# Where the cache slots start in SBUF, and which DMA engines take the last row of wo

## The chip, the cores and the metric

The kernel runs on one core of one Trainium2 chip. The metric is the device time of one execution, in microseconds (us), as the median of several. Executions of this kernel agree within about 0.1%.

## The reference

It is one decode step. The costly part is attention of one query token over a long cache; around it are two layer norms, a small MLP and a gate.

```python
B, Sq, D = 2, 1, 512
Hq, Hkv, Sk, Dh = 32, 8, 32768, 128       # k_cache, v_cache: [B, Hkv, Sk, Dh], bf16

q = (xn @ wq).reshape(B, Sq, Hq, Dh).transpose(0, 2, 1, 3)
k, v = repeat(k_cache, 4, axis=1), repeat(v_cache, 4, axis=1)
p = softmax(einsum("bhqd,bhkd->bhqk", q, k) * Dh ** -0.5)
s = einsum("bhqk,bhkd->bhqd", p, v).transpose(0, 2, 1, 3).reshape(B, Sq, Hq * Dh) @ wo
g = silu(mlp(xn))                          # mlp: w1 to w4 ... (cut)
return x + s * g
```

The two caches are 268 MB. Every byte is read once, so the kernel is a stream from HBM with some arithmetic beside it.

## The kernel before

Each load of the cache is 4 MB. It lands in one of five rotating "slots" of 32 KB in each of the 128 partitions. The same slots take wq, w3 with w4, and at the end wo. A pool gives its tiles addresses in the order in which pools are opened, so the 19 KB of small tiles in `pers` come first and the slots begin behind them.

```python
    pers = ctx.enter_context(tc.tile_pool(name="pers", bufs=1))
    slots = ctx.enter_context(tc.tile_pool(name="slots", bufs=SLOTS))     # SLOTS = 5
    ktp = ctx.enter_context(tc.tile_pool(name="ktp", bufs=T_BUFS))
    # ... more pools

    def slot(name):
        return slots.tile([128, SLOT], BF16, tag="slot", name=name)       # SLOT = 16384

    def load_cache(cache, b, g, i, name):
        t = slot(name)
        nc.sync.dma_start(
            out=t[:, :],
            in_=cache[b, g, i * NK:(i + 1) * NK, :].rearrange("(p t) d -> p (t d)", p=128),
        )
        return t
```

The prologue issues six loads one after another (wq, k0, k1, w3, w4, v0). From then on each load waits for a slot to be free.

```python
    wo_parts = [(0, RW // 2), (RW // 2, RW - 4), (RW - 4, RW - 1), (RW - 1, RW)]   # RW = 32
    for n in range(NW + 1):                   # NW = 32 pairs of k and v loads
        if n + 2 < NW:
            k_tiles[n + 2] = load_cache(A_k_cache, *work[n + 2], "k")
        if 0 < n + 1 < NW:
            v_tiles[n + 1] = load_cache(A_v_cache, *work[n + 1], "v")
        if n == NW - 1:
            wo_t = slot("wo")
            wo3 = wo_t[:, 0:Hq * D].rearrange("p (r c) -> p r c", r=RW)
            wos = A_wo.rearrange("(p r) d -> p r d", r=RW)
            for a, z in wo_parts:
                nc.sync.dma_start(out=wo3[:, a:z, :], in_=wos[:, a:z, :])
        # ... transposes, scores, exp, and the weighted sum of v
    # ... then 128 matmuls of oX with wo3, row by row, and the output
```

wo has 32 rows of 1 KB in each partition. It comes in four pieces of 16, 12, 3 and 1 rows, so that little is left to multiply once the last one lands.

The softmax here doesn't subtract the row's maximum and nothing guards it: scores larger than these inputs give would overflow.

Of the kernel before, what the change touches and what calls it, by code (L numbers as in the profile page):

```python
# [9 lines left out]
BF16 = mybir.dt.bfloat16  # L10
# [9 lines left out]
SLOTS = 5  # L20
# [6 lines left out]
def kernel(  # L27
# [14 lines left out]
    nc = tc.nc  # L42

    B, Sq, D = A_x.shape
# [18 lines left out]
    QW = D // NQ  # L63
    QP = 32 * (NQ - 1) + B
    RW = HD // 128
    RQ = Dh // RW

    pers = ctx.enter_context(tc.tile_pool(name="pers", bufs=1))
    slots = ctx.enter_context(tc.tile_pool(name="slots", bufs=SLOTS))
    ktp = ctx.enter_context(tc.tile_pool(name="ktp", bufs=T_BUFS))  # L70
    epp = ctx.enter_context(tc.tile_pool(name="epp", bufs=2))
    ptp = ctx.enter_context(tc.tile_pool(name="ptp", bufs=3))
# [7 lines left out]
    def slot(name):  # L80
        return slots.tile([128, SLOT], BF16, tag="slot", name=name)
# [8 lines that stand above are left out]
# [6 lines left out]
        out=wq_t[:, 0:DK * HD],  # L96
        in_=A_wq.rearrange("(p k) f -> p (k f)", k=DK),
    )

    x4_bf = pers.tile([128, QW], BF16)  # L100
    nc.gpsimd.memset(x4_bf[:, :], 0.0)
    for n in range(NQ):
        nc.gpsimd.dma_start(out=x4_bf[32 * n:32 * n + B, :], in_=A_x[:, 0, n * QW:(n + 1) * QW])
# [18 lines left out]
    for j in range(4):  # L122
        nc.vector.tensor_copy(
            out=sel[:, :, :, j, :],
            in_=ident[:, :].rearrange("p (b w e) -> p b e w", b=NB, e=2),
# [4 lines left out]
        out=sel_o[:, :, :],  # L130
        in_=ident[:, :].rearrange("p (j a t h) -> p a t h j", j=4, t=VT, h=rep)[:, 0, :, :, :],
# [4 lines left out]
        out=sel_h[:, :],  # L136
        in_=ident[:, :].rearrange("p (r h) -> p h r", h=rep),
# [4 lines left out]
    with nc.allow_low_precision(reason="sums of zeros and a single one"):  # L142
        nc.vector.tensor_reduce(
            out=sel_r[:, :],
            in_=ident[:, :].rearrange("p (q r) -> p r q", r=RW),
# [4 lines left out]
        out=mask[:, :],  # L150
        in_=ident[:, :].rearrange("p (q r) -> p q r", r=RW),
# [48 lines left out]

    onx = pers.tile([128, B, Hq, RQ], BF16)

    oX = pers.tile([128, RW, B], BF16)
    g4 = pers.tile([128, QW], F32)
    x4 = pers.tile([128, QW], F32)
    nc.gpsimd.tensor_copy(out=x4[:, :], in_=x4_bf[:, :])
# [14 lines left out]
    for nb in range(NB):  # L221
# [9 lines left out]
        out=qr[:, :, :, :, :].rearrange("p n e b h -> p (n e b h)"),  # L231
        in_=qr_ps[:, :, :, :].rearrange("p n e c -> p (n e c)"),
# [56 lines left out]
    def emit_k(n):  # L289
        b, g, i = work[n]  # L290
        if i == 0:
            state["z"] = emit_z(b, g)
        z = state["z"]
        kt = k_tiles.pop(n)[:, :].bitcast(I32)
        sc = sc_ps.tile([128, RT * 32], F32, tag="sc", name="sc")
        W = RT * NB * 32
        for r in range(NR):
            T = ktp.tile([128, W], I32, tag="T", name="T")
            nc.vector.transpose(  # L299
                out=T[:, :].rearrange("p (b t k) -> p t b k", b=NB, t=RT),  # L300
                in_=kt[:, r * W:(r + 1) * W].rearrange("p (t b k) -> p t b k", b=NB, t=RT),
            )
            Tb = T[:, :].bitcast(BF16).rearrange("p (b c e) -> p b c e", b=NB, e=2)
            zc = (NR - 1 - r) * rep
            for nb in range(NB):
                for e in range(2):
                    nc.tensor.matmul(  # L307
                        sc[:, :],
                        lhsT=z[:, nb, e, zc:zc + 128],
                        rhs=Tb[:, nb, :, e],  # L310
                        start=(r == 0 and nb == 0 and e == 0),
                        stop=(r == NR - 1 and nb == NB - 1 and e == 1),
                    )
        ep = epp.tile([128, RT * 32], BF16, tag="ep", name="ep")
        rs = smp.tile([128, 1], F32, tag="rs", name="rs")
        nc.scalar.activation(out=ep[:, :], in_=sc[:, :], func=ACT.Exp, scale=inv_sqrt_dh, accum_out=rs[:, :])  # L316
        pt = ptp.tile([128, NR, RT * rep], BF16, tag="pt", name="pt")
        nc.vector.transpose(  # L318
            out=pt[:, :, :].rearrange("p r (t h) -> p t r h", h=rep),
            in_=ep[:, :].rearrange("p (t r h) -> p t r h", r=NR, h=rep),  # L320
        )
        return pt, rs
# [46 lines left out]
                )  # L369
                nc.vector.tensor_copy(out=oX[:, :, b], in_=xp[:, :])  # L370

    wo_parts = [(0, RW // 2), (RW // 2, RW - 4), (RW - 4, RW - 1), (RW - 1, RW)]
    NW = len(work)
    eps = {}
    for n in range(NW + 1):
# [5 lines that stand above are left out]
            wo_t = slot("wo")  # L381
            wo3 = wo_t[:, 0:Hq * D].rearrange("p (r c) -> p r c", r=RW)
            wos = A_wo.rearrange("(p r) d -> p r d", r=RW)
            for a, z in wo_parts:
                nc.sync.dma_start(out=wo3[:, a:z, :], in_=wos[:, a:z, :])  # L385
        if n < NW:
            eps[n] = emit_k(n)
        if n == 1:
            emit_mlp()
        if n > 0:  # L390
            emit_v(n - 1, eps.pop(n - 1))
# [16 lines left out]
    for b, eng in ((0, nc.sync), (1, nc.scalar)):  # L408
        eng.dma_start(
            out=out[b, 0, :].rearrange("(n c) -> n c", c=QW),  # L410
            in_=out4[b:QP:32, :],
# [31 lines left out]
```

## Time and profile before

| | before |
|---|---|
| time, median | 665.06 us |
| span in the profile | 663.4 us |
| share of 16 DMA engines' span, queue of the loads | 98.6% |
| rate between 50 and 600 us | 431 GB/s |
| PE, DVE busy | 62%, 52% |
| where the slots start | 35872 B = 70 x 512 + 32 |

The address is from the built program. The slots are 32768 B apart, so all five start 32 B past a multiple of 512.

In the profiles PE is the engine of the matrix products and PEld its loading of weights; DVE, ACT and POOL are the vector, scalar and general engines, and SP issues the loads. A q after a name (SPq) is that engine's instruction queue. L307 is line 307 of the kernel. PEclk is the clock that PE was granted, as a share of full speed.

First the profile's page of the kernel before: part 1 gives the engines' busy time (and share of the span), part 2 the DMA's rate in 40 slices, part 3 the DMA queues with packets, MB and share of 16 engines, part 4 the chain of waits that ended last, by engine and line.

```profile
span 663.4 us, 6213 instructions
PE 411.3 (62%) x2622; PEld 172.7 (26%) x2622; DVE 344.8 (52%) x422; ACT 50.1 (8%) x152; POOL 7.0 (1%) x20
...
GB/s 380 419 433 440 428 426 437 427 432 435 422 435 428 431 434 429 430 435 428 433 431 428 433 426 435 432 427 434 427 434 431 424 437 430 425 439 428 429 430 203
...
q1 hardware_dynamic: 10232, 280.50, 98.6%
q8 instruction: 20, 0.33, 0.2%
...
DMA 75%; PE 16%; DVE 6%; issue 2%; ACT 0%; SPq 0%; DVEq 0%; ACTq 0%
DMA k<-in_A_k_cache_dram 69%; PE sc L307 13%; DMA wo<-in_A_wo_dram 6%; DVE T L299 5%; PE o L339 3%; DVE pt L318 1%; ACT ep L316 0%; PE S L335 0%; PE s_ps L397 0%; DVE sm L334 0%; SPq L95 0%; SPq L385 0%; DVE sg L405 0%; DVE out L407 0%; DVEq L299 0%
```

Read it from the queue: q1 has something to move nearly always, and no compute engine is close to full. The chain says the same. The windows table of the kernel before, for the long middle stretch, has the engines' busy time, the granted clock, the DMA share and GB/s as its last three numbers:

```profile
core 0: us, PE busy (x) PEld busy (x) DVE busy (x) ACT busy (x) POOL busy (x), PEclk, DMA share, GB/s
50.00:600.00 550.00, 351.12 (x2027) 142.63 (x2025) 293.98 (x346) 40.14 (x124) 0.00 (x0) 0.78 1.00 431
```

A DMA share of 1.00 means that the engines never idle here. Only two things can shorten this stretch: fewer bytes, or less time for each packet. The DMA issues of the kernel before show the four pieces of wo (KB each, then us from issue to landing), and the last steps of its chain show what follows the landing (start, us, what):

```profile
wo<-in_A_wo_dram SPq DMA_DIRECT2D x1, 2048.0 KB, 34.6
wo<-in_A_wo_dram SPq DMA_DIRECT2D x1, 1536.0 KB, 37.9
wo<-in_A_wo_dram SPq DMA_DIRECT2D x1, 384.0 KB, 38.4
wo<-in_A_wo_dram SPq DMA_DIRECT2D x1, 128.0 KB, 38.3
```

```profile
619.16 37.85 DMA wo<-in_A_wo_dram
657.01 0.04 issue
657.05 1.91 PE s_ps L397 x64
658.96 0.02 issue
658.98 0.30 DVE sg L405
```

Last, the packets themselves. The trace has one record for each, with queue, start, duration and size, but not the DMA engine; which packets share an engine is inferred, here and below, from one starting where another ends (within a few ns: most often 3 or 4 ns before it). Some 32 KB packets take 1.6 to 1.9 us: each of the 24 of them after the first 40 us starts within 20 ns of the end of an instruction packet (18 of queue q8, 6 of q14). These "interrupted" ones are left out. Counted over the others, more than 50 us after the first:

```
kernel before: 7757 packets, mean 1217.9 ns
  1216 ns 56%   1224 ns 22%   1215 ns 9%   1221 ns 6%   ...
before about 33 us: 338 of the uninterrupted ones take 1213 ns
```

### The profile page before, as it was taken

The page shows a single profiled execution, that of the slowest core. Times are in us where ns is not written, and L with a number is a line of the kernel's source. Part 1 is how long each engine was busy: PE and PEld are TensorE (multiplying, and loading weights), DVE is VectorE, ACT ScalarE, POOL GpSimd, SP SyncE. Part 2 cuts the span into 40 slices and gives each one's busy share as a digit, 9 for nine tenths or more (in the row PEclk, how much of TensorE's full clock was granted, in tenths as well). Part 3 has the DMA queues.
Part 4 walks back from the last instruction along what each step waited for, and adds up shares of the span by engine and source line. Part 5 has one row for each costly group of instructions (what it writes and reads, how often), then busy time and mean ns, then how long its engine had stood idle before and what let it go on. Part 6 is the DMA issues. An engine that isn't in the chain of part 4 may idle for free.

```text
span 663.4 us, 6213 instructions
## 1 busy us (share of the span) xinstructions
PE 411.3 (62%) x2622; PEld 172.7 (26%) x2622; DVE 344.8 (52%) x422; ACT 50.1 (8%) x152; POOL 7.0 (1%) x20
## 2 busy tenths in 40 slices
PE   2585667576468755567665655766565576764574
PEld 2242223222123322223222222322222232221222
DVE  4563456554445655445656444565644466554450
ACT  1111100000000000000000000000000000000000
POOL 3000000000000000000000000000000000000000
PEclk9985898667887867788876779887678987778886
DMA  9999999999999999999999999999999999999994
GB/s 380 419 433 440 428 426 437 427 432 435 422 435 428 431 434 429 430 435 428 433 431 428 433 426 435 432 427 434 427 434 431 424 437 430 425 439 428 429 430 203
DMA packets 10528, 280.89 MB, mean 423 GB/s; under 512 B 1403, under 2 KB 1541, under 8 KB 1669
## 3 DMA queue, kind: packets, MB, share of 16 engines
q1 hardware_dynamic: 10232, 280.50, 98.6%
q8 instruction: 20, 0.33, 0.2%
q0 software_dynamic: 256, 0.01, 0.0%
q14 instruction: 8, 0.06, 0.0%
q10 hardware_dynamic: 12, 0.00, 0.0%
HBM read 280.50 MB, written 0.00 MB: 423 GB/s over the span
## 4 chain that ended last, share of the span: by engine, by line
DMA 75%; PE 16%; DVE 6%; issue 2%; ACT 0%; SPq 0%; DVEq 0%; ACTq 0%
DMA k<-in_A_k_cache_dram 69%; PE sc L307 13%; DMA wo<-in_A_wo_dram 6%; DVE T L299 5%; PE o L339 3%; DVE pt L318 1%; ACT ep L316 0%; PE S L335 0%; PE s_ps L397 0%; DVE sm L334 0%; SPq L95 0%; SPq L385 0%; DVE sg L405 0%; DVE out L407 0%; DVEq L299 0%
## 5 line engine op out<-in xcount | busy, mean ns | idle before, releaser
L307 PE MATMUL sc<-T,z 128*128 128x512 bf16 x1024 | 300.4, 460 | 190.3 <-DVE T L299 190.0
L299 DVE STREAM_TRANSPOSE T<-k 128x1024 int32<-128x1024 int32 x256 | 292.1, 1208 | 178.3 <-DMA k<-in_A_k_cache_dram 178.3
L307 PEld LDWEIGHTS <-z 128*128 128x128 bf16 x1024 | 114.1, 111 | 375.1 <-issue 293.8
L339 PE MATMUL o<-v,pt 128*16 128x512 bf16 x1024 | 73.7, 439 | 4.7 <-DMA v<-in_A_v_cache_dram 4.7
L318 DVE STREAM_TRANSPOSE pt<-ep 128x512 bf16<-128x512 bf16 x32 | 22.8, 711 | 77.5 <-ACT ep L316 77.5
L316 ACT ACTIVATE ep<-sc 128x512 bf16<-128x512 f32 x32 | 19.1, 597 | 536.3 <-PE sc L307 536.3
L339 PEld LDWEIGHTS <-pt 128*16 128x16 bf16 x1024 | 25.5, 98 | 41.1 <-issue 23.7
L335 PE MATMUL S<-sm,ones_f 128*128 128x4 f32 x64 | 12.0, 258 | 24.8 <-DVE sm L334 24.8
L351 PE MATMUL oT<-sel_o,ob 128*128 128x4 f32 x128 | 16.9, 255 | 11.1 <-ACT ob L348 11.1
L351 PEld LDWEIGHTS oT<-sel_o,ob 128*128 128x128 f32 x128 | 15.5, 191 | 19.5 <-ACT ob L348 19.5
L335 PEld LDWEIGHTS S<-sm,ones_f 128*128 128x128 f32 x64 | 9.7, 190 | 32.6 <-DVE sm L334 32.6
L330 DVE MEMSET o<- 128x512 f32 x16 | 7.8, 485 | 13.4 <-ACT ob L348 12.3
L283 ACT COPY z<-qr 32x16 bf16<-32x16 bf16 x64 | 12.6, 197 | 11.5 <-DVE qr L230 10.9
L358 DVE TENSOR_TENSOR on<-oT,rec 128x4 f32<-128x4 f32 x16 | 2.6, 162 | 20.0 <-PE oT L351 20.0
L348 ACT COPY ob<-o 128x512 f32<-128x512 f32 x16 | 9.4, 585 | 26.0 <-PE o L339 26.0
L356 DVE RECIPROCAL rec<-S 128x4 f32<-128x4 f32 x16 | 2.9, 183 | 7.3 <-PE S L335 7.2
L212 PE MATMUL qT_ps<-xT,wq 128*128 128x2 bf16 x128 | 3.6, 165 | 4.5 <-DMA wq<-in_A_wq_dram 4.5
L316 ACT ACTIVATION_READ_ACCUMULATOR ep<-sc 128x1 f32 x32 | 6.3, 198 | 0.2
L334 DVE TENSOR_SCALAR sm<-sel_h,rs 128x4 f32<-128x4 f32 x32 | 6.1, 189 | 0.0
L212 PEld LDWEIGHTS <-wq 128*128 128x128 bf16 x128 | 3.5, 104 | 4.6 <-DMA wq<-in_A_wq_dram 4.6
L195 PE MATMUL treg<-ident,xn_bf 2*128 2x2 bf16 x4 | 0.3, 175 | 6.8 <-DVE xn_bf L187 6.8
L397 PE MATMUL s_ps<-wo,oX 128*2 128x128 bf16 x128 | 3.0, 265 | 1.7 <-DMA wo<-in_A_wo_dram 1.4
(63 smaller groups left out, 42.0 us busy)
## 6 DMA issues: line engine op xcount, KB each, us to landing
k<-in_A_k_cache_dram SPq DMA_DIRECT2D x32, 4096.0 KB, 44.3
v<-in_A_v_cache_dram SPq DMA_DIRECT2D x32, 4096.0 KB, 39.4
wq<-in_A_wq_dram SPq DMA_DIRECT2D x1, 4096.0 KB
w<-in_B_w_dram SPq DMA_DIRECT2D x2, 1792.0 KB, 37.8
wo<-in_A_wo_dram SPq DMA_DIRECT2D x1, 2048.0 KB, 34.6
wo<-in_A_wo_dram SPq DMA_DIRECT2D x1, 1536.0 KB, 37.9
wo<-in_A_wo_dram SPq DMA_DIRECT2D x1, 384.0 KB, 38.4
wo<-in_A_wo_dram SPq DMA_DIRECT2D x1, 128.0 KB, 38.3
```

Source lines behind the costliest of these rows:

```text
L212: nc.tensor.matmul(qT_ps[:, h * B:(h + 1) * B], lhsT=wq3[:, k, h * Dh:(h + 1) * Dh], rhs=xT[:, k, :], start=(k == 0), stop=(k == DK - 1),)
L283: nc.scalar.copy(out=z[32 * j:32 * j + 32, :, :, c:c + rep], in_=qr[32 * j:32 * j + 32, :, :, b, g * rep:(g + 1) * rep],)
L299: nc.vector.transpose(out=T[:, :].rearrange("p (b t k) -> p t b k", b=NB, t=RT), in_=kt[:, r * W:(r + 1) * W].rearrange("p (t b k) -> p t ...
L307: nc.tensor.matmul(sc[:, :], lhsT=z[:, nb, e, zc:zc + 128], rhs=Tb[:, nb, :, e], start=(r == 0 and nb == 0 and e == 0), stop=(r == NR - 1 ...
L316: nc.scalar.activation(out=ep[:, :], in_=sc[:, :], func=ACT.Exp, scale=inv_sqrt_dh, accum_out=rs[:, :])
L318: nc.vector.transpose(out=pt[:, :, :].rearrange("p r (t h) -> p t r h", h=rep), in_=ep[:, :].rearrange("p (t r h) -> p t r h", r=NR, h=rep),)
L330: nc.vector.memset(state["o"][:, :], 0.0)
L334: nc.vector.tensor_scalar_mul(out=sm[:, :], in0=sel_h[:, :], scalar1=rs[:, 0:1])
L335: nc.tensor.matmul(S[:, :], lhsT=ones_f[:, :], rhs=sm[:, :], start=(i == 0), stop=(i == NPART - 1))
L339: nc.tensor.matmul(o[32 * j:32 * j + VT * rep, :], lhsT=pt[:, r, a * VT * rep:(a + 1) * VT * rep], rhs=vt[:, u * VT:(u + 1) * VT, :].rearr ...
L348: nc.scalar.copy(out=ob[:, :], in_=o[:, :])
L351: nc.tensor.matmul(oT[:, :], lhsT=ob[:, t * Dh:(t + 1) * Dh], rhs=sel_o[:, t, :], start=(t == 0), stop=(t == VT - 1),)
```

## The change

It has two parts. The first moves all of `pers` behind the slots and leaves a small pool, `head`, ahead of them. `head` holds 256 + 128 = 384 B, which brings the slots to 16896 = 33 x 512. The second splits the last piece of wo by partitions, 119 and 9, so that the DMA engines share this row unequally. The intent is shorter packets in the stream, and less work at the end for the engines that finish last.

```diff
+    head = ctx.enter_context(tc.tile_pool(name="head", bufs=1))
+    slots = ctx.enter_context(tc.tile_pool(name="slots", bufs=SLOTS))
     pers = ctx.enter_context(tc.tile_pool(name="pers", bufs=1))
-    slots = ctx.enter_context(tc.tile_pool(name="slots", bufs=SLOTS))
 ...
-    x4_bf = pers.tile([128, QW], BF16)
+    x4_bf = head.tile([128, QW], BF16)
 ...
-    oX = pers.tile([128, RW, B], BF16)
+    oX = head.tile([128, RW, B], BF16)
 ...
-    wo_parts = [(0, RW // 2), (RW // 2, RW - 4), (RW - 4, RW - 1), (RW - 1, RW)]
+    wo_parts = [
+        (0, RW // 2, 0, 128), (RW // 2, RW - 4, 0, 128), (RW - 4, RW - 1, 0, 128),
+        (RW - 1, RW, 0, 119), (RW - 1, RW, 119, 128),
+    ]
 ...
-            for a, z in wo_parts:
-                nc.sync.dma_start(out=wo3[:, a:z, :], in_=wos[:, a:z, :])
+            for a, z, p0, p1 in wo_parts:
+                nc.sync.dma_start(out=wo3[p0:p1, a:z, :], in_=wos[p0:p1, a:z, :])
```

## The prediction

What the prediction says of the hardware and no trace or run of this case shows is cut; the cuts are marked. The sum: 665.06 - 0.34 - 0.3 = 664.4 us, put at 664.2 for the chance of a larger effect of alignment. The grounds of its two terms:

- The 0.34 us of the tail rest on an assumption: that the seven engines which take the 119 partitions are the seven that end early. Each later engine would then have eight 1 KB packets less to write. In the trace of the kernel before, such packets are 46 ns long and follow each other on an engine about 43 ns apart, and eight are 0.34 us. If the assumption fails, the prediction had the change 0.4 us slower.
- Why an off start should cost anything was not shown, so this term, 0 to 1 ns per packet, is the author's estimate. The larger case, a gain of 2 to 4 us (661 to 663 us), is the one in which the later 3 and 8 ns per packet come from the off start.

> **What bounds the kernel now.** The DMA stream. The DMA table gives the cache loads' queue 98.6% of 16 engines' span; the windows table has DMA share 1.00 and 431 GB/s from 50 to 600 us, while PE is busy 62% and DVE 52% of the span (page, part 1). The chain of waits is 75% DMA. 280.5 MB at 431 GB/s is 651 of the 663.4 us.
>
> **The packets (trace's DMA records).** Each cache load is 128 packets of 32 KB, one per partition. Before about 33 us they take 1213 ns, later 1216 ns, with 1221 or 1224 ns about every fourth descriptor. Packets of 1, 3, 14 and 32 KB in the quiet phase took 46, 121, 535 and 1213 ns: a slope of 27.2 GB/s per engine (435 GB/s for 16), plus about 8 ns each. At that slope 32 KB is 1205 ns. So what is not payload in the steady stream is about 84 ns of the 9.72 us that one load takes on each engine: 0.9%, under 6 us over 67 loads. Alignment can give no more.
>
> **Alignment.** As built, every slot starts 32 B past a multiple of 512. [...] But the trace says it costs little: [...] the slots were as misaligned while packets took 1213 ns as later. I expect 0 to 1 ns less per packet, about 0.3 us in all, with some chance of 2 to 4 us[...].
>
> **The last row of wo.** Following packet chains, the engines end their last wo packets between 653 and 658 us: seven within the first microsecond, nine 3 to 5 us later, three of these in the last 0.3 us. The late ones carry more interruptions by instruction packets (16 KB, 1.07 us). [...] 0.34 us off the last to end, all on the critical path.
>
> **Sum.** 665.06 - 0.34 (tail) - 0.3 (alignment) = 664.4; with the chance of a larger alignment effect I say 664.2 us, range 662.0 to 665.2. Faster by over 2%: 0.01; within 2%: 0.98; slower: 0.01.
>
> **What would show it.** Tail: the last row's 1 KB packets on seven engines, the last engine 0.3 us earlier, the early seven 0.4 us later. Alignment: 32 KB packets still at 1213 early and 1216/1224 later, 431 GB/s mid-run. If alignment matters more, the common packet falls towards 1205 to 1213 ns and mid-run shows 433 GB/s or above.
>
> **What would make it wrong.** [...] instruction fetches landing elsewhere and moving the last engine by up to 1 us.

## The result, and the profile after

| | before | after |
|---|---|---|
| time, median | 665.13 us (665.03 to 665.48, 6 runs) | 662.20 us (662.04 to 662.58, 6 runs) |
| span in the profile | 663.4 us | 660.5 us |
| 32 KB packets, mean after the first 50 us | 1217.9 ns | 1213.0 ns |
| instruction packets of 16 KB (q8), median | 1071 ns | 935 ns |
| rate between 50 and 600 us | 431 GB/s | 433 GB/s |

The ratio is 0.9956, with a 95% interval of 0.9943 to 0.9968. A ratio here is the mean time of one kernel's runs over that of the other's of the same rounds, so it is not quite the ratio of the medians. The change saves 2.9 us, 0.4%. By the rule of 2% that is "same", but it is clear of the noise.

The page of the kernel after, the same parts:

```profile
span 660.5 us, 6182 instructions
PE 408.5 (62%) x2590; PEld 173.7 (26%) x2622; DVE 344.9 (52%) x422; ACT 50.1 (8%) x152; POOL 6.9 (1%) x20
...
GB/s 381 418 437 442 416 442 435 425 442 429 430 439 422 439 440 421 440 433 426 443 429 426 443 426 433 434 429 438 433 428 439 426 435 440 425 435 438 427 428 210
...
q1 hardware_dynamic: 10232, 280.50, 98.6%
q8 instruction: 20, 0.33, 0.2%
...
DMA 75%; PE 15%; DVE 6%; issue 2%; ACT 0%; SPq 0%; DVEq 0%; ACTq 0%
```

The shares did not move: 98.6% and 75% as before. This is how a faster stream looks when the stream is the limit. Only the rate tells, in the windows table of the kernel after:

```profile
50.00:600.00 550.00, 347.68 (x1999) 143.18 (x2026) 294.81 (x348) 40.83 (x126) 0.00 (x0) 0.77 1.00 433
```

DVE is busy as long as before (344.9 us against 344.8), so the moved tiles changed nothing for it. (PE has 2590 matmul records in place of 2622: some are missing from this trace.) The DMA issues and the end of the chain of the kernel after:

```profile
wo<-in_A_wo_dram SPq DMA_DIRECT2D x1, 2048.0 KB, 34.3
wo<-in_A_wo_dram SPq DMA_DIRECT2D x1, 1536.0 KB, 37.7
wo<-in_A_wo_dram SPq DMA_DIRECT2D x1, 384.0 KB, 38.3
wo<-in_A_wo_dram SPq DMA_DIRECT2D x1, 119.0 KB
```

```profile
617.69 38.15 DMA wo<-in_A_wo_dram
655.84 0.04 issue
655.88 0.30 PE s_ps L402 x4
656.19 0.02 issue
656.21 0.30 DVE sg L410
```

Before, the chain left the DMA with 64 matmuls to do: it waited last for the piece of 12 rows, which is 48 matmuls and is followed by 16 more. The last row was not on the chain. It was issued at 620.1 us and landed 38.3 us later, at 658.4, while its own four matmuls start only at 658.6: it had some 0.25 us in hand. After, only 4 matmuls remain, which are those of the split row. That row has become what ends last.

The packet records of the kernel after are unlike those before: 7757 uninterrupted packets of 32 KB, and to the nearest percent all of them take 1213 ns, and so do the earlier ones from about 6 us on. (In the first microseconds, as all engines start, packets are longer and scattered in both kernels, up to 2.1 us before and 2.4 us after.) The 1216 and 1224 ns are gone.

### The profile page after: what moved, and what is told of

It is laid out like the page before. It is cut to its first block, busy times and chain, and to the rows that moved or that the text cites. A ratio compares the mean times of both kernels' runs of the same rounds, so it can differ in the third digit from the quotient of the medians.

```text
span 660.5 us, 6182 instructions
## 1 busy us (share of the span) xinstructions
PE 408.5 (62%) x2590; PEld 173.7 (26%) x2622; DVE 344.9 (52%) x422; ACT 50.1 (8%) x152; POOL 6.9 (1%) x20
## 3 DMA queue, kind: packets, MB, share of 16 engines
q1 hardware_dynamic: 10232, 280.50, 98.6%
## 4 chain that ended last, share of the span: by engine, by line
DMA 75%; PE 15%; DVE 6%; issue 2%; ACT 0%; SPq 0%; DVEq 0%; ACTq 0%
DMA k<-in_A_k_cache_dram 69%; PE sc L309 11%; DMA wo<-in_A_wo_dram 6%; DVE T L301 6%; PE o L341 3%; DVE pt L320 1%; ACT ep L318 0%; PE S L337 0%; SPq L390 0%; DVE sm L336 0%; SPq L97 0%; PE s_ps L402 0%; DVE sg L410 0%; DVE out L412 0%; DVEq L301 0%
## 5 line engine op out<-in xcount | busy, mean ns | idle before, releaser
L309 PE MATMUL sc<-T,z 128*128 128x512 bf16 x992 | 295.2, 457 | 190.6 <-DVE T L301 183.3
L341 PE MATMUL o<-v,pt 128*16 128x512 bf16 x1024 | 75.5, 447 | 4.9 <-DMA v<-in_A_v_cache_dram 4.9
## 6 DMA issues: line engine op xcount, KB each, us to landing
wo<-in_A_wo_dram SPq DMA_DIRECT2D x1, 384.0 KB, 38.3
```

The source lines that it names most:

```text
L309: nc.tensor.matmul(sc[:, :], lhsT=z[:, nb, e, zc:zc + 128], rhs=Tb[:, nb, :, e], start=(r == 0 and nb == 0 and e == 0), stop=(r == NR - 1 ...
L341: nc.tensor.matmul(o[32 * j:32 * j + VT * rep, :], lhsT=pt[:, r, a * VT * rep:(a + 1) * VT * rep], rhs=vt[:, u * VT:(u + 1) * VT, :].rearr ...
```

## The experiments

Eleven kernels ran, each correct. In the table, the ratio is to the kernel before in the same rounds. "Packet" is the mean of the uninterrupted 32 KB packets more than 50 us after the first.

| run | slots mod 512 | last rows of wo | time, us (median) | ratio | packet, ns |
|---|---|---|---|---|---|
| before (665.13 to 665.33 in the four sets) | 32 | not split | 665.14 | 1 | 1217.9 |
| after | 0 | 1 row, 119 + 9 | 662.20 | 0.9956 | 1213.0 |
| align_only | 0 | not split | 662.07 | 0.9953 | 1213.0 |
| split_only | 32 | 1 row, 119 + 9 | 665.56 | 1.0005 | 1217.9 |
| order_only | 32 | not split | 665.29 | 1.0001 | 1217.9 |
| pad_only | 0 | not split | 662.09 | 0.9952 | 1213.0 |
| off_256 | 256 | not split | 661.86 | 0.9948 | 1213.0 |
| off_128 | 128 | not split | 664.54 | 0.9989 | 1216.9 |
| off_64 | 64 | not split | 664.56 | 0.9989 | 1216.8 |
| wq_pieces | 32 | not split | 665.02 (one run) | | see text |
| four_rows | 0 | 4 rows, 119 + 9 | 664.58 | 0.9991 | 1213.0 |
| row_124 | 0 | 1 row, 124 + 4 | 662.21 | 0.9957 | 1213.0 |
| row_122 | 0 | 1 row, 122 + 6 | 662.17 | 0.9956 | 1213.0 |

### The two parts, one at a time

Theory A says that the start of the slots is the whole gain and that the split row costs a little. Rivals: the split is the gain (B), both help (C), or what helps is the new order of the pools and not the address (D). The first four ran in one set of five rounds. The later sets ran on other chips, each with the kernel before beside it.

**align_only**: the change with the old four pieces of wo.

```diff
# against the kernel after, in effect
-        (RW - 1, RW, 0, 119), (RW - 1, RW, 119, 128),
+        (RW - 1, RW, 0, 128),
```

> The change's slot placement (slots at a multiple of 512 B) with the old four wo pieces. Theory A (the slot start is the whole gain, through shorter packets; the split of the last row sits on three of the late engines and costs time): 661.8 us, a little faster than the full change's 662.2, common packet 1213 ns throughout. Rival B (the gain is the split row): as before, 665.1. Rival C (both help, as the prediction had it, 0.34 us from the split): 662.5.

Measured: 662.07 us (661.56 to 662.13), ratio 0.9953 (0.9939 to 0.9967). The address alone gives 3.07 us.

**split_only**: the kernel before with the five new pieces of wo.

```diff
# against the kernel before
-    wo_parts = [..., (RW - 4, RW - 1), (RW - 1, RW)]
+    wo_parts = [..., (RW - 4, RW - 1, 0, 128), (RW - 1, RW, 0, 119), (RW - 1, RW, 119, 128)]
```

> The kernel before with only the last row of wo split into 119 and 9 partitions; slots stay at 32 mod 512. Theory A: 665.5 us, 0.4 slower than before, since three of the late engines get ten more 1 KB packets each; packets still 1216/1224 after 33 us. Prediction (the seven engines are the early ones): 664.8. Rival B: 662.2.

Measured: 665.56 us (665.33 to 665.84), ratio 1.0005 (0.9993 to 1.0018). The median is 0.42 us above that of before, the number of theory A; the interval includes 1, so this run by itself does not settle a difference of this size. Nor does its trace show theory A's way to the number. The steps at the end of its chain:

```profile
619.24 38.21 DMA wo<-in_A_wo_dram
657.45 0.04 issue
657.50 2.03 PE s_ps L400 x64
```

With 64 matmuls to follow, what PE waits for last is again the piece of 12 rows and not the last row, and that piece landed at 657.45 us in place of 657.01. Its packets had become slower, as is shown under "The split row" below. So the size agreed with theory A by luck. (This trace is of the slowest of the five runs, 665.84 us.)

**order_only**: align_only with one more tile of 32 B in `head`, so the new pool order with slots at 32 mod 512.

```diff
     head = ctx.enter_context(tc.tile_pool(name="head", bufs=1))
+    pad = head.tile([128, 16], BF16, name="pad")
```

> align_only with 32 B more ahead of the slots: the pool order of the change, but slots at 32 mod 512 as before. Theory A (the start address alone): back to 665.1 us and packets of 1216/1224 ns. Rival D (what counts is that the small tiles moved behind the slots, or which tiles share which region): stays at 661.8.

Measured: 665.29 us (665.15 to 665.45), ratio 1.0001. The whole gain is gone with 32 B.

**pad_only**: the pool order of before, with 480 B of padding.

```diff
     pers = ctx.enter_context(tc.tile_pool(name="pers", bufs=1))
+    pad = pers.tile([128, 240], BF16, name="pad")
```

> The pool order of before, with 480 B of padding so that slots start at 0 mod 512; old wo pieces. Theory A: 661.8 us, packets of 1213 ns throughout. Rival D: 665.1.

Measured: 662.09 us (661.84 to 662.11), ratio 0.9952. The whole gain is there without any reordering. These two runs decide against D: in both directions the time follows the address. The windows table shows it too; here is order_only and then pad_only:

```profile
50.00:600.00 550.00, 348.40 (x2015) 141.87 (x2015) 294.00 (x346) 40.15 (x124) 0.00 (x0) 0.78 1.00 431
```

```profile
50.00:600.00 550.00, 347.51 (x2035) 142.29 (x2039) 294.39 (x345) 40.84 (x126) 0.00 (x0) 0.79 1.00 433
```

### Which multiple is needed

Each of these is align_only with a tile of 256, 128 or 64 B more in `head`, three rounds in one set. In the three expectations the first number is for the case that a start at a multiple of 256 B is enough (off_256), that one of 256 or 512 B is needed (off_128), or one of 128 B or more (off_64).

```diff
     head = ctx.enter_context(tc.tile_pool(name="head", bufs=1))
+    pad = head.tile([128, 128], BF16, name="pad")      # off_256; 64 for off_128, 32 for off_64
```

> Slots at 256 mod 512, pool order of the change, old wo pieces. [...] 662.0 us, packets 1213 ns throughout. If the change's 512 B is what is needed: 665.1 us and packets of 1216/1224 ns after 33 us.

Measured: 661.86 us, ratio 0.9948 (0.9933 to 0.9963), every packet 1213 ns. A multiple of 256 B is enough; 512 is not needed.

> Slots at 128 mod 512. [...] 665.1 us, packets 1216/1224. If a start at a multiple of 64 or 128 B is enough: 662.0, 1213.

Measured: 664.54 us, ratio 0.9989 (0.9972 to 1.0006), mean packet 1216.9 ns.

> Slots at 64 mod 512. [...] 665.1 us, packets 1216/1224. If 64 B is enough (32 is the only odd one): 662.0, 1213.

Measured: 664.56 us, ratio 0.9989 (0.9975 to 1.0004), mean packet 1216.8 ns. So 64 and 128 B lose most of the gain. Both are 0.8 us better by the median than 32 B. The intervals include 1, but each of their eight runs is faster than each of the seven of the kernel before, and their packets are 1 ns better, which goes the same way: 485 packets on each engine at 1 ns are 0.5 us. At 128 B a fifth of the packets still take 1213 ns. Neither expectation had this step between.

The extra per packet, over 1213.0 ns, is 4.9 ns at 32 B, 3.8 at 64 and 3.9 at 128, and none at 256. So it does not grow with the offset. The source in HBM is unchanged in these runs; only the destination in SBUF moves. Why an off start costs time is not shown.

### What turns the cost on at 33 us

In the kernel before, the same misaligned slots cost nothing at first: the first loads are at 1213 ns, and engine after engine changes to the slower pattern between about 33 and 40 us. One engine is ahead of the others: followed from packet to packet, it is the one that an instruction packet interrupted at 18.4 us, and its packets take mostly 1219 ns from 22.3 us and 1214 to 1224 ns from 27.2 us. **wq_pieces** is the kernel before with its first load cut in four. The 64th descriptor of its expectation follows from the traces: a load of 128 packets is eight on each of 16 engines, and the eighth load is issued at 33.40 us in the kernel before and at 4.47 us here.

```diff
-    nc.sync.dma_start(out=wq_t[:, 0:DK * HD], in_=A_wq.rearrange("(p k) f -> p (k f)", k=DK))
+    for k in range(DK):
+        nc.sync.dma_start(
+            out=wq_t[:, k * HD:(k + 1) * HD],
+            in_=A_wq.rearrange("(p k) f -> p k f", k=DK)[:, k, :],
+        )
```

> The kernel before (slots at 32 mod 512) with the first load, wq, issued as four loads of 8 KB rows, so nine DMAs are issued in the first 5 us in place of six. It asks what turns the extra cost on at 33 us. If it is the number of descriptors handed to the queue (the 64th per engine is handed over with the eighth DMA, then at 33.4 us, now by 5 us), k0 and k1 already show 1216/1224 ns. If it is the compute engines' traffic to SBUF (VectorE begins on the first cache load at 24 us), k0 and k1 stay at 1213 ns and the change still comes at about 33 us. Time within 1 us of before, 664.5 to 666.

Measured in one look: 665.02 us, of unknown state. The engines now change over between about 14 and 29 us, while k0 and k1 land. VectorE starts on the first cache load at 24.26 us, against 24.25 in the kernel before, and nearly all engines have changed over by then; so its traffic is not the trigger. More descriptors (a descriptor is the order for one packet) brought the change earlier, and the early engine above had an instruction packet more than the others, so their count may play a part; that is argued from one look each. But the version that was put to the test, the 64th descriptor handed to the queue, would have had it by 5 us, and it does not come then. What the trigger is stays open.

### The split row

In the trace of after, two engines take exactly one 1 KB packet of the last row, and seven take long runs of them, seventeen rows and one (not split, its 128 packets are eight on each of 16). Of the seven, four are among the first to end (650.8 to 651.4 us) and three are among the last. Counted from the start of the span, the three end their runs at about 654.3, 655.1 and 655.3 us; the last engine without such rows ends at 654.5. So the engines that were relieved are not the last ones, and the two that end last were loaded.

**four_rows**: align_only with its last four rows split this way.

```diff
-    (RW - 4, RW - 1), (RW - 1, RW)
+    (RW - 4, RW, 0, 119), (RW - 4, RW, 119, 128)
```

No trace numbers engines. In this expectation and the next two, passages that rest on such numbers are cut. "Those" are the loaded engines of theory A, seven as in the trace of after, with ten more 1 KB packets per row: 0.43 us at 43 ns. The other number supposes them all early, and 0.34 us less per row on the late ones.

> align_only with its last four rows of wo (not only one) split into 119 and 9 partitions: the cost of the split, fourfold. Theory A [...]: each row costs 0.43 us on those, so 662.0 + 4 x 0.43 = 663.7 us. The prediction's reading [...]: 660.6.

Measured: 664.58 us (664.32 to 665.28), which is 2.5 us over align_only's 662.07, in another set. The sign is theory A's, and the size is larger than its 1.7. The profile shows another way to it. The DMA issues of align_only first, then of four_rows:

```profile
wo<-in_A_wo_dram SPq DMA_DIRECT2D x1, 2048.0 KB, 34.2
wo<-in_A_wo_dram SPq DMA_DIRECT2D x1, 1536.0 KB, 37.5
```

```profile
wo<-in_A_wo_dram SPq DMA_DIRECT2D x1, 2048.0 KB, 35.2
wo<-in_A_wo_dram SPq DMA_DIRECT2D x1, 1536.0 KB, 39.6
```

The 1536 KB piece is the same DMA in both kernels, on all 128 partitions, and it lands 2.1 us later in four_rows; 1.0 us of that is there already at the 2048 KB piece before it. Neither is queued behind the split rows. The packets themselves have become slow:

```
12 KB packets of wo (128 in each kernel)      mean     over 1.1 x median   longest
before                                        465.3 ns         0            472 ns
split_only                                    482.0           23            605
align_only                                    460.0            0            460
after                                         462.6            2            569
row_122                                       463.9            5            547
row_124                                       466.6           11            544
four_rows                                     535.6           34            874
```

The first two have slots at 32 mod 512, the others at 0. So a transfer that is spread over seven engines (four in row_124, two in row_122) slows the other engines while they still write their own pieces. The slowing is measured; what causes it is not shown.

**row_124** and **row_122** ask whether another split would help: in their traces the 124 partitions go to four engines and the 122 to two.

```diff
-        (RW - 1, RW, 0, 128),
+        (RW - 1, RW, 0, 124), (RW - 1, RW, 124, 128),      # row_124
+        (RW - 1, RW, 0, 122), (RW - 1, RW, 122, 128),      # row_122
```

"These four" are the four loaded engines. The first time is for the case that all of them end early, the second for one of them late. The terms are the author's estimate, at 43 ns for a packet.

> align_only with the last row of wo split into 124 and 4 partitions[...] These four gain 24 packets of 43 ns, 1.03 us, the twelve lose 0.34 us. [...] 661.7 us. If one of them is among the late ones: 662.0 + 1.0 = 663.0.

Measured: 662.21 us (662.10 to 662.78), neither 661.7 nor 663.0. The last packet in its trace is one of the split row, 0.3 us later than the last packet of align_only. The time alone does not tell which of the two cases holds, but the trace does: three of the four loaded engines end by 651.9 us, and the fourth ends last of all, at 655.0. So one of the four belongs to the late group. The split does not help.

"Engines 0 and 1" is the author's name for the two loaded engines of row_122; that they end early was assumed. The terms are an estimate at 43 ns for a packet.

> align_only with the last row of wo split into 122 and 6 partitions[...] Engines 0 and 1 gain 54 packets, 2.3 us, which fits the slack; the others lose 0.30 to 0.34 us. Expected 661.7 us; if engines 0 and 1 are late after all, 664.3.

Measured: 662.17 us (662.12 to 662.67); no gain either. The split row is done early here, by 653.6 us, so the engines that took it are not the last. The others have seven or eight packets fewer. Yet the piece of three rows ahead of it, on all 128 partitions, ends at 655.0 us in place of align_only's 654.3, and 15 of its 128 packets are over 1.1 times the median, against none. The slowing is there again, but it is not all: the engine that ends last in row_122 was 0.5 us behind already at the end of its 16 KB packets, none of which is slow, and on it the 12 KB packets cost only 0.14 us more (3.79 us in place of 3.65 for the eight). The two traces are of row_122's slowest run (662.67) and align_only's fastest (661.56). How much of the missing gain is due to slower packets is not shown. As before, PE waits last for the piece of 12 rows, so relief in the row after it had little to give.

No version beats align_only clearly. align_only, pad_only and off_256, at 661.9 to 662.1 us, are within each other's spread, and 0.1 to 0.3 us under the whole change, in other sets of rounds.

## Why the prediction was right or wrong

**The time.** 662.20 us lies in the range of 662.0 to 665.2, near its lower end and 2.0 us under the point of 664.2. The gain was about three times the predicted 0.9 us. It is the width of the range that holds the result: its lower end was set by a case that was thought unlikely.

**What bounds the kernel: right.** The stream still has a DMA share of 1.00, and a shorter packet went into the time nearly in full.

**The ceiling for alignment: right.** Under 6 us was possible, and 3.07 us came (align_only). The 8 ns that each packet costs beyond its bytes are still there with aligned slots: a 32 KB packet takes 1213 ns, not 1205.

**The alignment term: mis-sized.** The step that failed reads "the slots were as misaligned while packets took 1213 ns as later. I expect 0 to 1 ns less per packet, about 0.3 us in all". The premise was correct, and the conclusion does not follow from it: the cost of the off start was there only once something else had turned it on (1213 ns before about 33 us, mostly 1216 and 1224 after). Measured is 4.9 ns per packet. The sum then comes out: 485 packets of 32 KB on each engine at 4.9 ns are 2.4 us; the packets of w3, w4 and wo, which became up to 5 ns shorter, give another 0.1 us. The instruction packets went from 1071 to 935 ns, so an engine that was interrupted two or three times in the stream gains some 0.3 us; that is an estimate from the count of 20 such packets and of nine late engines. Together that is 2.8 of the 3.07 us. The rest is not assigned.

**The prediction named this case**: "some chance of 2 to 4 us", with 1213 ns and 433 GB/s or above as its signs. Exactly these signs were seen, though no run shows the mechanism. The case was given too little weight.

**The last row of wo: wrong in sign.** The failing step took the seven engines that the 119 partitions go to for the seven that end early. That was assumed and not shown. In the trace after, four of the seven loaded engines are early and three are late. A second step failed with it: "0.34 us off the last to end, all on the critical path". In the kernel before, PE waited last for the piece of 12 rows, which landed at 657.0 us, and had 64 matmuls to do from there; the last row landed at 658.4, about 0.25 us before PE came to it. By this trace, taking work from that row could not have saved time, whichever engines took it. On misaligned slots the split cost 0.42 us by the medians (the interval includes no difference), not the gain of 0.34; on aligned slots 0.13 us, which is within the noise; with four rows 2.5 us. The prediction also left out that the split slows the packets of other engines, those of the 12-row piece that PE does wait for among them: it landed 0.44 us later in split_only.

## What to carry to other kernels

When a load stream has a DMA share of 1.00, look at the duration of single packets. Here values a few ns above the common one of the start (1216 and 1224 over 1213 ns) were time to be had, and they went away when the destination in SBUF began at a multiple of 256 B (1213.0 ns at 0 and 256 B mod 512; 1216.8 to 1217.9 at 128, 64 and 32). It costs one padding tile to try. That a condition was present from the start while its cost was not does not acquit it; compare with a version in which it is absent. And check which piece the end waits for, and which engines end last, before work is moved between them. A transfer on fewer than 16 engines also slowed the others here (12 KB packets of up to 874 ns in four_rows, 460 in align_only).
